# Spectral mixing and SiLU block: the first transform stage folds rows m and 47 - m, and runs as sixteen products between two pairs of chunks

## The chip, the core and the metric

The kernel runs on one core of one Trainium2 chip. The metric is the time of one execution in microseconds (us), measured on the device; a kernel's time is the median of its runs. The profile is one execution of the program, recorded by the hardware profiler. In it PE is the matmul engine (TensorE), PEld its loading of stationary operands, DVE the vector engine, ACT the scalar engine, POOL the GpSimd engine; SPq, ACTq and POOLq are those engines issuing DMA transfers.

## What is computed

```python
# x: (8, 3008, 256) fp32; filt_r, filt_i: (1505, 256); w_in: (256, 2048); w_out: (2048, 256)
X = np.fft.rfft(x, axis=1)                     # 3008 = 94 * 32 points, for each batch and channel
Y = X * (filt_r + 1j * filt_i)[None]
y = np.fft.irfft(Y, n=3008, axis=1)
x = y.reshape(24064, 256)
h = x @ w_in
g = h * (1.0 / (1.0 + np.exp(-h)))             # SiLU
out = g @ w_out
```

Everything is fp32. The forward transform is done in two stages: the first over 94 points (94 rows, 32 n' apart) for each of the 32 values of n', the second over the 32 n'. The two matrix products are done with seven products of quarters instead of eight (a Strassen scheme), which is where the tables A11, A12, S1 to S4 and A22 come from.

## The kernel before

The main loop has 8 batches x 48 steps. A step is one eighth of the hidden units (`NJP = 8`) of one pair of chunks of tokens; six pairs make a batch. A step has eight rounds. In each step `hidden` issues seven products for the first matrix and `project` seven for the second, for the step before. All four `acc` banks of a pair are copied out (`drain`) at the end of its eighth `project`.

```python
def hidden(step):                      # rounds 0 to 7, "yield" ends a round
    mm(xo, A11, yt[:, 0, 0:n], True);  nc.scalar.copy(out=sums[:, 0, 0:n], in_=xo)
    yield
    mm(zo, A12, yt[:, 1, 0:n], True);  combine(v, g[:, 0, 0:n], zo, sums[:, 0, 0:n], ALU.add)
    finish()                           # g[:, 6] and g[:, 7] of the step before
    yield
    mm(xo, S2, t[:, 2, 0:n], False);   nc.scalar.copy(out=sums[:, 1, 0:n], in_=xo);  silu(0)
    yield
    mm(yo, S1, t[:, 0, 0:n], True)
    yield
    mm(xo, S3, t[:, 1, 0:n], False);   nc.scalar.copy(out=sums[:, 2, 0:n], in_=xo)
    combine(v, g[:, 2, 0:n], yo, sums[:, 2, 0:n], ALU.add)
    yield
    yield
    mm(xo, A22, t[:, 3, 0:n], False);  silu(3, xo);  silu(2)
    yield
    mm(yo, S4, yt[:, 1, n:2 * n], False)
    combine(v, g[:, 1, 0:n], yo, sums[:, 1, 0:n], ALU.add);  silu(1)
    combine(v, g[:, 4:6, 0:n], g[:, 1:3, 0:n], g[:, 0:2, 0:n], ALU.subtract)
# drain(pair, i): acc bank i -> s, by ACT for even i and DVE for odd i; after i = 3 seven sums on GpSimd
```

The transform of batch b is cut into pieces, which are placed among the main loop's steps of the batch before (`put(step, round, piece)`; a piece is issued after that round's products). The pieces of the forward transform:

```python
def load_x(u):                         # u = 0..7: four n', rows 0..46 of both halves
    xs[u] = x_t[u % 2]                 # two tiles [128, 2, 2, C]
    for h in range(2):
        for r0, nr in ((0, 32), (32, N1 - 32)):
            queue.dma_start(out=xs[u][64 * h + r0:64 * h + r0 + nr], in_=...)

def sums(u):                           # even residues take the sum of the halves, odd ones the difference
    for par, op in ((0, ALU.add), (1, ALU.subtract)):
        nc.vector.tensor_tensor(out=ut[0:111, par], in0=xt[0:111, 0], in1=xt[0:111, 1], op=op)
    if b > 0 and u + 2 < 8:
        load_x(u + 2)

def stage1(u):                         # four products of 47 rows x 64 columns, 512 wide
    for par in range(2):
        for h in range(2):
            rows = slice(64 * h, 64 * h + N1)
            nc.tensor.matmul(out=ps[h][64 * par:64 * par + 64], lhsT=wf_t[rows, par],
                             rhs=ut[rows, par], start=True, stop=True)
    for h in range(2):
        evac(t1[:, h], ps[h])          # DVE and ACT by turns
    for par in range(2):
        nc.gpsimd.dma_start(out=d1[par]..., in_=t1[...])     # to DRAM, in transposed order

def forward(g):                        # second stage, g = 0..5: sixteen products of 64 x 32, 256 wide
    ...                                # load_t2(g) brings d1 back before it
def multiply(g, k): ...                # two DVE products 128x512 with the filter
def add(g, k): ...                     # two DVE sums 128x256
def inverse(g, n):                     # n = 2: thirty-two products of 32 x 64, 256 wide
    ps = [bank(b, f"pc_{b}_{g}_{j}", j // 2 if j % 2 == 0 else None) for j in range(4)]
    ...                                # two of its four banks are acc banks 0 and 1, free between two pairs
def even(g, i, n): ...                 # ACT copies bank 2 i out
def rows(g, i, n): ...                 # two DVE sums 128x512
def stage3(g): ...                     # last stage, g = 0..7: products of 48 x 64, 47 wide, two copies to y
```

```python
def plan(b, part):                     # b = 1..7
    at = STEPS * b                     # STEPS = 48
    put(at - 51, 0, part["load_x"], 0);  put(at - 51, 0, part["load_x"], 1)
    for u in range(8):
        put(at + u - (48 if u else 49), 5, part["sums"], u)
        put(at + u - 47, 3, part["stage1"], u)
    put(at - 39, 0, part["load_t2"], 0);  put(at - 39, 0, part["load_t2"], 1)
    ... # forward, multiply, add of g = 0..5 from -38 to -18
    for g, step in ((0, -32), (2, -24), (4, -16)):           # between two pairs of chunks
        put(at + step, 7, part["inverse"], g, 2)
        put(at + step, 7, part["even"], g, 0, 2)
        put(at + step + 1, 0, part["even"], g, 1, 2)
        put(at + step + 1, 5, part["rows"], g, 0, 2)
        put(at + step + 2, 3, part["rows"], g, 1, 2)
    ... # stage3: four at -11, -9, -6, -3, four at 9, 12, 15, 18
```

Batch 0 is transformed ahead of the main loop, together with the preparation of the weights.

Of the kernel before, what the change touches and what calls it, by code (L numbers as in the profile page):

```python
# [86 lines left out]
def dft_tables():  # L90

    wf = np.zeros((128, 2, 64))
    for par in range(2):
        for i, idx in enumerate(ORDER):
            ph = 2 * np.pi * (np.arange(N1) * (2 * idx + par) % 94) / 94
            for h in range(2):
                wf[64 * h:64 * h + N1, par, 2 * i] = np.cos(ph)
                wf[64 * h:64 * h + N1, par, 2 * i + 1] = -np.sin(ph)


    d = np.zeros((2, 2, 32, NS, 2, 32))
    n = np.arange(32)[:, None]
    for par in range(2):
        for i, idx in enumerate(ORDER):
            sp = 2 * idx + par
            kap = kept(sp)
            sg = np.where((kap - sp) % 94 == 0, 1.0, -1.0)
            k = np.where((kap - sp) % 94 == 0, kap, S - kap)
            th = 2 * np.pi * (n * k % S) / S
            d[par, 0, :, i, 0], d[par, 1, :, i, 0] = np.cos(th), np.sin(th)  # L110
            d[par, 0, :, i, 1], d[par, 1, :, i, 1] = -np.sin(th) * sg, np.cos(th) * sg


    e = np.zeros((4, 32, NG, 2, 2, 2, 32))
    n = np.arange(32)[None, :]
    for g in range(NG):
        for bank in range(2):
            for j in range(4):
                s = slot_residue(g, bank, j - j % 2)
                kap = kept(slot_residue(g, bank, j))  # L120
                sg = np.where((kap - s) % N1 == 0, 1.0, -1.0)[:, None]
                k = np.where((kap - s) % N1 == 0, kap, S - kap)[:, None]
                assert ((k - s) % 94 == (0 if j % 2 == 0 else N1)).all()
                th = 2 * np.pi * (n * k % S) / S
                e[j, :, g, bank, 0, 0], e[j, :, g, bank, 0, 1] = np.cos(th), np.sin(th)
# [12 lines left out]
    return (wf.astype(f32), wi.astype(f32), d.reshape(128, NS, 2, 32).astype(f32),  # L138
            e.reshape(128, NG, 2, 2, 64).astype(f32))


# [1 line left out]
def kernel(  # L143
# [9 lines left out]
    nc = tc.nc  # L153
    ctx.enter_context(tc.manual_schedule())

    wf_host, wi_host, d_host, e_host = dft_tables()
    wf_dram = nc.inline_tensor(wf_host, name="wf_tbl")
    wi_dram = nc.inline_tensor(wi_host, name="wi_tbl")
    d_dram = nc.inline_tensor(d_host, name="d_tbl")
    e_dram = nc.inline_tensor(e_host, name="e_tbl")  # L160
# [22 lines left out]
    accps = pool("accps", 1, PSUM)  # L183

    wf_t = cpool.tile([128, 2, 64], FP32)
    wi_t = cpool.tile([128, N1], FP32)
    d_t = cpool.tile([128, NS, 2, 32], FP32)
    e_t = cpool.tile([128, NG, 2, 2, 64], FP32)
# [2 lines left out]
    w_t = cpool.tile([128, 7, 2, NJP, 128], FP32)  # L191
    warm = cpool.tile([128, 1], FP32)
    bias_t = cpool.tile([128, 1], FP32)
    x_t = [xpool.tile([128, 2, 2, C], FP32, name=f"x{i}") for i in range(2)]

    def load_filters(first, last):
        for j in range(4):
# [35 lines left out]
    def spectral(b):  # L233
# [32 lines left out]
        def sums(u):  # L266
            if b > 0 or u % 3 == 0:
                ut = upool.tile([128, 2, 512], FP32, name=f"u_{b}_{u}", tag="u")
            else:
                if u == 1:  # L270
                    us["s"] = spool.tile([128, 2, 2, 512], FP32, name="u_s", tag="s")
                ut = us["s"][:, u % 3 - 1]
            xt = xs.pop(u)
            for par, op in ((0, ALU.add), (1, ALU.subtract)):
                nc.vector.tensor_tensor(out=ut[0:111, par], in0=xt[0:111, 0], in1=xt[0:111, 1], op=op)  # L275
            us[u] = ut
            if b > 0 and u + 2 < 8:
                load_x(u + 2)

        def stage1(u):  # L280
            ut = us.pop(u)
            if b > 0 or u < 2 or u > 5:
                t1 = tpool.tile([128, 2, 2, C], FP32, name=f"t1_{b}_{u}", tag="t")
            elif u < 4:
                t1 = typool.tile([128, 2, 2, C], FP32, name=f"t1_{b}_{u}", tag="ty")
            else:
                t1 = us["t1"][:, u - 4]
            ps = [bank(b, f"pa_{b}_{u}_{h}") for h in range(2)]
# [6 lines that stand above are left out]
                evac(t1[:, h], ps[h])  # L295
            for par in range(2):
                nc.gpsimd.dma_start(  # L297
                    out=d1[par].rearrange("s p n c -> (s p) n c")[:, 4 * u:4 * u + 4, :],
                    in_=t1[64 * par:64 * par + 2 * NS].rearrange("p h n c -> p (h n) c"))

        def load_t2(g):
            t2s[g] = tpool.tile([128, 4, C], FP32, name=f"t2_{b}_{g}", tag="t")
# [77 lines left out]
        def stage3(g):  # L380
# [17 lines left out]
            for h in range(2):  # L398
                evac(dst[:, :, h, n0:n0 + 4], ps[h])

        return dict(load_x=load_x, sums=sums, stage1=stage1, load_t2=load_t2, forward=forward,
                    multiply=multiply, add=add, inverse=inverse, even=even, rows=rows, load_t4=load_t4, stage3=stage3)

    pending = []

    def put(step, rnd, piece, *args):

        pending.append((step + rnd / ROUNDS, len(pending), lambda: piece(*args)))

    def plan(b, part):  # L410

        at = STEPS * b

        put(at - 51, 0, part["load_x"], 0)
        put(at - 51, 0, part["load_x"], 1)
        for u in range(8):
            put(at + u - (48 if u else 49), 5, part["sums"], u)
            put(at + u - 47, 3, part["stage1"], u)
        put(at - 39, 0, part["load_t2"], 0)
        put(at - 39, 0, part["load_t2"], 1)  # L420

        for g, places in enumerate((
# [6 lines left out]
            pieces = (("forward", g), ("multiply", g, 0), ("multiply", g, 1), ("add", g, 0), ("add", g, 1))  # L429
            for (step, rnd), (piece, *args) in zip(places, pieces):  # L430
                put(at + step, rnd, part[piece], *args)
        for g, step in ((0, -32), (2, -24), (4, -16)):

            put(at + step, 7, part["inverse"], g, 2)
            put(at + step, 7, part["even"], g, 0, 2)
            put(at + step + 1, 0, part["even"], g, 1, 2)
            put(at + step + 1, 5, part["rows"], g, 0, 2)
            put(at + step + 2, 3, part["rows"], g, 1, 2)
        put(at - 14, 5, part["load_t4"], 0)
        for g, step in enumerate((-11, -9, -6, -3)):  # L440
            put(at + step, 3, part["stage3"], g)
        plan_rest(b, part)

    def plan_rest(b, part):

        for g, (step, rnd) in enumerate(((9, 3), (12, 6), (15, 6), (18, 6))):
            put(STEPS * b + step, rnd, part["stage3"], 4 + g)

    pairs = [(b, half, c0, n) for b in range(B) for half in range(2) for c0, n in PAIRS]
# [228 lines left out]

    nc.sync.dma_start(out=wf_t, in_=wf_dram.ap())
    nc.gpsimd.memset(bias_t, -896.0)  # L680
    part = spectral(0)
    for u in range(8):
        part["load_x"](u)
# [14 lines left out]
    for g in range(NG):  # L698
        part["forward"](g)
        if g == 0:  # L700
            load_filters(4, 2 * NG)
            nc.sync.dma_start(out=wi_t, in_=wi_dram.ap())
        if g < 3:
            weights(1 + g)
        for k in range(2):
            part["multiply"](g, k)
        for k in range(2):
            part["add"](g, k)
        if 2 <= g < NG - 1:
            rounded(g)  # L710
        if g > 0:
            inverse_rows(part, g - 1)
# [18 lines left out]
    per = len(PAIRS) * 2  # L731


    combines = ((-2, 1), (6, 1), (14, 5), (22, 5), (26, 6), (38, 1))
    stores = (((10, 1), (10, 5)), ((19, 1), (23, 5)), ((31, 1), (31, 5)), ((35, 1), (35, 5)),
              ((43, 1), (43, 5)), ((50, 1), (51, 1)))
    for pair in range(len(pairs)):
# [55 lines left out]
```

## Time and profile before

| | |
|---|---|
| time, median of 3 runs | 2670.82 us (2669.16 to 2671.6) |
| span of the profiled execution | 2669.7 us |
| main loop starts (first `px<-y` product) | at 127.71 us |
| `pa` (first stage) matmul records, `L292` | 512 |
| DVE, `u<-x` sums, `L275` | 118 of mean 715 ns |
| `d<-t` transfers to DRAM issued by GpSimd, `L297` | 124, 526 ns each, 3.0 us to landing |
| `x<-in_x_dram` transfers issued by SP | 240, median 2.9 us (128 KB) and 2.7 us (60 KB) to landing |

A fp32 product appears in the profile as two records. A line of the timeline gives the start, the time until the last of its records ends, the engine, the line of the program, the operation, out<-in by tile names, the shape, and how many records were merged; records of PE overlap, so their durations must not be added up. What counts for PE is the distance from one start to the next. A window line gives a stretch of the span and, for each engine, its busy time and number of instructions, then the granted PE clock and the DMA engines' mean share and rate.

### The profile page before, as it was taken

The numbers are of one execution on the slowest core, as the hardware profiler recorded it, in microseconds if no ns is written. First come the engines' busy times: TensorE is split into PE (matmuls) and PEld (weight loads), VectorE is DVE, ScalarE is ACT, GpSimd is POOL, SyncE is SP. The second block draws the span as 40 slices with busy tenths as digits, with TensorE's granted clock in tenths as the row PEclk, the third lists the DMA queues.
The fourth block names the chain that finished last, engine by engine and source line by source line (L and its number), as shares of the span: only waits on it lengthen the run. The fifth ranks groups of instructions, "written<-read, shape, count | busy, mean of one in ns | idle before, by whom it ended". The sixth has DMA issues, their size and how long they took to land.

```text
span 2669.7 us, 47316 instructions
## 1 busy us (share of the span) xinstructions
PE 2582.3 (97%) x18432; PEld 2165.9 (81%) x18432; DVE 1683.3 (63%) x3554; ACT 1099.8 (41%) x3000; POOL 448.1 (17%) x653
## 2 busy tenths in 40 slices
PE   4589999999999999999999999999999999999998
PEld 1268888788887888888887888878888788888987
DVE  4886765667566665666656676566756667555554
ACT  1244444444444444444444444444444444444443
POOL 3541111211111111111101111021111111100100
PEclk9599999999999999999999999999999999999999
DMA  9732121421224211331123311132122421211000
GB/s 211 190 104 64 56 50 38 106 55 37 56 59 101 50 28 48 86 88 41 36 60 81 70 56 47 41 100 59 40 56 47 108 56 26 50 28 21 9 16 16
DMA packets 203616, 166.26 MB, mean 62 GB/s; under 512 B 120896, under 2 KB 175808, under 8 KB 203264
## 3 DMA queue, kind: packets, MB, share of 16 engines
q1 hardware_dynamic: 184728, 111.11, 18.6%
q0 software_dynamic: 14992, 47.46, 5.8%
q10 hardware_dynamic: 3672, 4.67, 0.7%
q8 instruction: 145, 2.38, 0.4%
q14 instruction: 79, 0.65, 0.1%
HBM read 88.17 MB, written 74.97 MB: 61 GB/s over the span
## 4 chain that ended last, share of the span: by engine, by line
PE 93%; DVE 2%; DMA 2%; SPq 1%; issue 1%; ACT 1%; POOL 0%; DVEq 0%; ACTq 0%
PE acc L543 42%; PE px L484 25%; PE pyz L484 18%; PE pd L391 3%; PE pa L292 2%; PE pb L315 2%; PE pc L348 2%; SPq L203 1%; DMA x<-in_x_dram 1%; DMA t<-d 1%; DVE g L455 0%; DMA d<-q 0%; DVE u L275 0%; DMA filt<-in_filt_i_dram 0%; DVE q L367 0%
## 5 line engine op out<-in xcount | busy, mean ns | idle before, releaser
L543 PE MATMUL acc<-g,w_t 128*128 128x256 f32 (+1 forms) x5376 | 1513.1, 375 | 0.4 <-DVE g L455 0.4
L543 PEld LDWEIGHTS acc<-g,w_t 128*128 128x128 f32 x5376 | 1022.2, 190 | 116.0 <-DVE g L455 0.8
L455 DVE TENSOR_TENSOR g<-pyz,abc 128x256 f32<-128x256 f32 (+1 forms) x1152 | 479.6, 416 | 553.9 <-ACT abc L505 321.3
L455 DVE TENSOR_TENSOR g<-g 128x256 f32<-128x256 f32 (+3 forms) x1152 | 617.4, 536 | 196.7 <-ACT g L488 183.6
L484 PE MATMUL px<-ty,w_t 128*128 128x256 f32 (+1 forms) x2304 | 690.3, 381 | 4.2 <-ACT abc L499 3.7
L488 ACT ACTIVATE g<-g 128x256 f32<-128x256 f32 (+1 forms) x1152 | 472.9, 411 | 231.6 <-DVE g L455 231.6
L484 PEld LDWEIGHTS px<-ty,w_t 128*128 128x128 f32 x2304 | 422.1, 190 | 118.5 <-issue 58.0
L455 POOL TENSOR_TENSOR s<-s 128x256 f32<-128x256 f32 (+1 forms) x329 | 259.1, 805 | 1318.5 <-DVE s L561 1262.3
L484 PE MATMUL pyz<-y,w_t 128*128 128x256 f32 (+1 forms) x1536 | 455.3, 378 | 1.7 <-DVE g L455 1.7
L484 PEld LDWEIGHTS pyz<-y,w_t 128*128 128x128 f32 x1536 | 283.3, 190 | 45.1 <-DVE g L455 5.6
L499 ACT COPY abc<-px 128x256 f32<-128x256 f32 (+1 forms) x384 | 141.5, 369 | 371.4 <-PE px L484 371.4
L488 ACT ACTIVATE g<-px 128x256 f32<-128x256 f32 (+1 forms) x384 | 146.1, 380 | 308.3 <-PE px L484 308.3
L505 ACT COPY abc<-px 128x256 f32<-128x256 f32 (+1 forms) x384 | 143.2, 373 | 296.1 <-PE px L484 295.9
L484 PE MATMUL px<-y,w_t 128*128 128x256 f32 (+1 forms) x768 | 228.8, 380 | 3.6 <-ACT g L488 2.7
L484 PE MATMUL pyz<-ty,w_t 128*128 128x256 f32 (+1 forms) x768 | 225.4, 375 | 0.7 <-DVE g L455 0.7
L484 PEld LDWEIGHTS px<-y,w_t 128*128 128x128 f32 x768 | 143.3, 190 | 29.2 <-issue 11.1
L484 PEld LDWEIGHTS pyz<-ty,w_t 128*128 128x128 f32 x768 | 145.5, 190 | 18.3 <-DVE g L455 1.8
L492 ACT COPY abc<-px 128x256 f32<-128x256 f32 (+1 forms) x384 | 134.9, 351 | 2.7 <-PE px L484 1.3
L213 DVE COPY y<-pd 128x376 f32<-128x376 f32 x64 | 51.3, 807 | 101.1 <-PE pd L391 101.1
L297 POOL DMA_DIRECT2D d<-t x124 | 64.7, 526 | 293.6 <-ACT abc L505 278.0
L391 PEld LDWEIGHTS pd<-wi_t,t 48*64 48x64 f32 x4096 | 69.5, 140 | 36.5 <-issue 29.2
L315 PE MATMUL pb<-t,d_t 64*32 64x256 f32 x1536 | 61.2, 408 | 37.4 <-DMA t<-d 18.9
(52 smaller groups left out, 1284.4 us busy)
## 6 DMA issues: line engine op xcount, KB each, us to landing
t<-d SPq DMA_DIRECT2D x96, 256.0 KB, 3.9
t<-d SPq DMA_DIRECT2D x128, 192.0 KB, 3.6
d<-t POOLq DMA_DIRECT2D x124, 192.0 KB, 3.0
d<-q POOLq DMA_DIRECT2D x85, 256.0 KB, 2.6
out_dram<-o SPq DMA_DIRECT2D x636, 32.0 KB, 1.8
x<-in_x_dram SPq DMA_DIRECT2D x120, 128.0 KB, 2.9
x<-in_x_dram SPq DMA_DIRECT2D x120, 60.0 KB, 2.7
raw<-in_moe_w_in_dram SPq DMA_DIRECT2D x16, 256.0 KB, 6.3
```

The source lines that it names most:

```text
L292: nc.tensor.matmul(out=ps[h][64 * par:64 * par + 64], lhsT=wf_t[rows, par], rhs=ut[rows, par], start=True, stop=True)
L297: nc.gpsimd.dma_start(out=d1[par].rearrange("s p n c -> (s p) n c")[:, 4 * u:4 * u + 4, :], in_=t1[64 * par:64 * par + 2 * NS].rearrange(" ...
L315: nc.tensor.matmul(out=ps[k][32 * j:32 * j + 32, ri, :], lhsT=d_t[rows, 4 * g + at, ri, :], rhs=t2[rows, at, :], start=True, stop=True)
L348: nc.tensor.matmul(out=ps[j][64 * k:64 * k + 64, a, :], lhsT=e_t[rows, g + a, k, ri, :], rhs=zs[k][rows, ri, :], start=(a == 0 and ri == 0 ...
L391: nc.tensor.matmul(out=ps[h][c0:c0 + 64, cb, i, :], lhsT=t4s[g][rows, i, 128 * cb + c0:128 * cb + c0 + 64], rhs=wi_t[rows, :], start=True, ...
L455: eng.tensor_tensor(out=out, in0=in0, in1=in1, op=op)
L484: nc.tensor.matmul(out=out, lhsT=w_t[:, c, 0, jp], rhs=rhs, start=start, stop=True, skip_group_check=True)
L488: nc.scalar.activation(out=g[:, k, 0:n], in_=g[:, k, 0:n] if src is None else src, func=AFT.Silu)
L492: nc.scalar.copy(out=sums[:, 0, 0:n], in_=xo)
L499: nc.scalar.copy(out=sums[:, 1, 0:n], in_=xo)
L505: nc.scalar.copy(out=sums[:, 2, 0:n], in_=xo)
L543: nc.tensor.matmul(out=acc[pair][i][:, h, 0:n], lhsT=w_t[:, c, 1, jp], rhs=g[:, k, 0:n], start=(jp == 0 and h == 0), stop=last, skip_group ...
```

## The change

From batch 2 on, six of the eight groups of four n' of the first stage are done in another way. The 94-point transform of real data has a symmetry: rows m and 47 - m have the same cosine and, but for the sign, the same sine. So rows m (0 to 23) and 47 - m are first summed and subtracted, and the product then needs 24 rows instead of 47. Four quarters of the partitions each hold two n', so that eight n' are done at a time (`f` = 0, 1, 2) with sixteen products of 24 rows x 32 columns: four sets of rows (`q`) times four tables (`k`: even and odd residues, cosine and sine). The remaining eight n' (`u` = 6, 7) stay as before, and so does the whole of batch 1.

The purpose is to have fewer passes through the matmul engine, and to have these passes between two pairs of chunks, where the accumulator banks 0 and 1 are free.

```diff
+    wq = np.zeros((128, 4, 32))                 # cosine and sine tables of 24 rows, for four quarters
...
-    x_t = [xpool.tile([128, 2, 2, C], FP32, name=f"x{i}") for i in range(2)]
+    x_all = xpool.tile([128, 2, 2, 2 * C], FP32)
+    x_t = [x_all[:, i] for i in range(2)]
...
-            if b > 0 and u + 2 < 8:
+            if b == 1 and u + 2 < 8:
                 load_x(u + 2)
...
+        def reverse_x():                        # DRAM to DRAM: rows 47 - m in the order of m
+            us["xr"] = dpool.tile([2, 24, 32 * C], FP32, name=f"xr_{b}", tag="xr")
+            nc.sync.dma_start(out=us["xr"][:, 1:24], in_=bass.AP(..., ap=[[32 * N1 * C, 2], [-32 * C, 23], [1, 32 * C]]))
+            for k in range(2):
+                nc.sync.dma_start(out=us["xr"][k, 0:1], in_=...)
+
+        def load_fold(f):                       # eight transfers
+            for q in range(4):
+                rows = slice(32 * q, 32 * q + 24)
+                nc.sync.dma_start(out=x_all[rows, 0], in_=...)         # rows m, two n'
+                nc.sync.dma_start(out=x_all[rows, 1], in_=us["xr"]...) # rows 47 - m
+
+        def fold(f, k):                         # k = 0..3
+            used = slice(0, 120)
+            if k == 0:
+                us["f"] = upool.tile([128, 2, 512], FP32, name=f"uf_{b}_{f}", tag="u")
+            xt, ut = x_all[used], us["f"][used]
+            todo = (((ut, xt[:, :, 0], xt[:, :, 1], ALU.add),),
+                    ((xt[:, :, 1], xt[:, :, 0], xt[:, :, 1], ALU.subtract),),
+                    ((xt[:, 0, 0], ut[:, 0], ut[:, 1], ALU.add),
+                     (xt[:, 1, 0], ut[:, 0], ut[:, 1], ALU.subtract)),
+                    ((ut[:, 0], xt[:, 0, 1], xt[:, 1, 1], ALU.subtract),
+                     (ut[:, 1], xt[:, 0, 1], xt[:, 1, 1], ALU.add)))
+            for out, in0, in1, op in todo[k]:
+                nc.vector.tensor_tensor(out=out, in0=in0, in1=in1, op=op)
+
+        def stage1_fold(f):
+            ut = us.pop("f")
+            rhs = x_all[:, 0, 0], x_all[:, 1, 0], ut[:, 0], ut[:, 1]
+            ps = [bank(b, f"pf_{b}_{f}_{q}", (0, 1, None, None)[q]) for q in range(4)]
+            for k in range(4):
+                for q in range(4):
+                    rows = slice(32 * q, 32 * q + 24)
+                    nc.tensor.matmul(out=ps[q][32 * k:32 * k + 32], lhsT=wq_t[rows, k], rhs=rhs[k][rows],
+                                     start=True, stop=True)
+
+        def evict_fold(f, q):
+            copy = nc.scalar.copy if q < 2 else nc.vector.tensor_copy
+            copy(out=us["tf"][:, q % 2], in_=us["ps"][q])
+            if q % 2:
+                for k in range(4):
+                    nc.gpsimd.dma_start(out=d1[k // 2, :, k % 2, n0:n0 + 4], in_=us["tf"][32 * k:32 * k + NS]...)
...
+        if b == 1:
             ...                                 # as before
+        else:
+            put(at - 72, 0, part["reverse_x"])
+            for f, step, load, places in ((0, -56, -66, ((-60, 3), (-60, 5), (-59, 5), (-58, 5))),
+                                          (1, -48, -55, ((-52, 3), (-52, 5), (-51, 5), (-50, 5))),
+                                          (2, -40, -44, ((-42, 5), (-41, 3), (-41, 5), (-40, 3)))):
+                put(at + load, 0, part["load_fold"], f)
+                for k, (fold_step, rnd) in enumerate(places):
+                    put(at + fold_step, rnd, part["fold"], f, k)
+                put(at + step, 7, part["stage1_fold"], f)
+                put(at + step, 7, part["evict_fold"], f, 0)
+                put(at + step + 1, 0, part["evict_fold"], f, 1)
+                put(at + step + 1, 5, part["evict_fold"], f, 2)
+                put(at + step + 1, 5, part["evict_fold"], f, 3)
+            for u, step in ((6, -46), (7, -45)):
+                put(at - 47, 0, part["load_x"], u)
+                put(at + step, 5, part["sums"], u)
+                put(at + step + 1, 3, part["stage1"], u)
-        put(at - 39, 0, part["load_t2"], 0)
+        put(at - 37, 0, part["load_t2"], 0)     # and of g = 1
-                ((-38, 3), (-37, 3), (-37, 5), (-36, 3), (-36, 5)),
-                ((-35, 3), (-35, 5), (-34, 3), (-33, 2), (-33, 5)),
+                ((-36, 3), (-36, 5), (-35, 3), (-35, 5), (-34, 5)),
+                ((-35, 6), (-34, 3), (-33, 3), (-33, 5), (-32, 1)),
...
-        for g, (step, rnd) in enumerate(((9, 3), (12, 6), (15, 6), (18, 6))):
+        for g, (step, rnd) in enumerate(((10, 3), (11, 3), (16, 3), (18, 6))):
             put(STEPS * b + step, rnd, part["stage3"], 4 + g)
...
+    nc.gpsimd.memset(x_all[96:128], 0.0)        # ahead of everything, in the preparation
+            nc.sync.dma_start(out=wq_t, in_=wq_dram.ap())
...
-    combines = ((-2, 1), (6, 1), (14, 5), (22, 5), (26, 6), (38, 1))
+    combines = ((-2, 1), (6, 1), (11, 5), (22, 5), (26, 6), (38, 1))
```

More of the change, by code (lines that the diff above doesn't have):

```diff
@@ L98, in dft_tables @@
                 wf[64 * h:64 * h + N1, par, 2 * i + 1] = -np.sin(ph)
+    wq = np.zeros((128, 4, 32))
+    m = np.arange(24)
+    for par in range(2):
+        for i, idx in enumerate(ORDER):
+            ph = 2 * np.pi * (m * (2 * idx + par) % 94) / 94
+            for q in range(4):
+                wq[32 * q:32 * q + 24, 2 * par, i] = np.where(m == 0, 0.5, np.cos(ph))
+                wq[32 * q:32 * q + 24, 2 * par + 1, i] = -np.sin(ph)
     d = np.zeros((2, 2, 32, NS, 2, 32))
@@ L137, in dft_tables @@
     f32 = np.float32
-    return (wf.astype(f32), wi.astype(f32), d.reshape(128, NS, 2, 32).astype(f32),
+    return (wf.astype(f32), wq.astype(f32), wi.astype(f32), d.reshape(128, NS, 2, 32).astype(f32),
             e.reshape(128, NG, 2, 2, 64).astype(f32))
@@ L154 @@
     ctx.enter_context(tc.manual_schedule())
-    wf_host, wi_host, d_host, e_host = dft_tables()
+    wf_host, wq_host, wi_host, d_host, e_host = dft_tables()
     wf_dram = nc.inline_tensor(wf_host, name="wf_tbl")
+    wq_dram = nc.inline_tensor(wq_host, name="wq_tbl")
     wi_dram = nc.inline_tensor(wi_host, name="wi_tbl")
@@ L185 @@
     wf_t = cpool.tile([128, 2, 64], FP32)
+    wq_t = cpool.tile([128, 4, 32], FP32)
     wi_t = cpool.tile([128, N1], FP32)
@@ L299, in stage1 @@
                     in_=t1[64 * par:64 * par + 2 * NS].rearrange("p h n c -> p (h n) c"))
+        def reverse_x():
+            us["xr"] = dpool.tile([2, 24, 32 * C], FP32, name=f"xr_{b}", tag="xr")
+            at = x.offset + b * S * C
+            nc.sync.dma_start(out=us["xr"][:, 1:24],
+                              in_=bass.AP(tensor=x.tensor, offset=at + 46 * 32 * C,
+                                          ap=[[32 * N1 * C, 2], [-32 * C, 23], [1, 32 * C]]))
+            for k in range(2):
+                nc.sync.dma_start(out=us["xr"][k, 0:1],
+                                  in_=bass.AP(tensor=x.tensor, offset=at + (1 - k) * 32 * N1 * C,
+                                              ap=[[32 * C, 1], [1, 32 * C]]))
@@ new lines, in load_fold @@
+        def load_fold(f):
+            at = x.offset + (b * S + 8 * f) * C
+            for q in range(4):
+                rows = slice(32 * q, 32 * q + 24)
+                n0 = (8 * f + 2 * q) * C
+                nc.sync.dma_start(out=x_all[rows, 0],
+                                  in_=bass.AP(tensor=x.tensor, offset=at + 2 * q * C,
+                                              ap=[[32 * C, 24], [32 * N1 * C, 2], [1, 2 * C]]))
+                nc.sync.dma_start(out=x_all[rows, 1],
+                                  in_=us["xr"][:, :, n0:n0 + 2 * C].rearrange("k m n -> m k n"))
@@ new lines, in stage1_fold @@
+        def stage1_fold(f):
[3 more added lines that the diff above has]
+            for k in range(4):
+                for q in range(4):
+                    rows = slice(32 * q, 32 * q + 24)
+                    nc.tensor.matmul(out=ps[q][32 * k:32 * k + 32], lhsT=wq_t[rows, k], rhs=rhs[k][rows],
+                                     start=True, stop=True)
+            us["ps"] = ps
@@ new lines, in evict_fold @@
+        def evict_fold(f, q):
+            if q % 2 == 0:
+                us["tf"] = tpool.tile([128, 2, 2, C], FP32, name=f"tf_{b}_{f}_{q}", tag="t")
+            copy = nc.scalar.copy if q < 2 else nc.vector.tensor_copy
+            copy(out=us["tf"][:, q % 2], in_=us["ps"][q])
+            if q % 2:
+                n0 = 8 * f + 2 * q - 2
+                for k in range(4):
+                    nc.gpsimd.dma_start(
+                        out=d1[k // 2, :, k % 2, n0:n0 + 4],
+                        in_=us["tf"][32 * k:32 * k + NS].rearrange("p q n c -> p (q n) c"))
@@ L399, in stage3 @@
                 evac(dst[:, :, h, n0:n0 + 4], ps[h])
-        return dict(load_x=load_x, sums=sums, stage1=stage1, load_t2=load_t2, forward=forward,
-                    multiply=multiply, add=add, inverse=inverse, even=even, rows=rows, load_t4=load_t4, stage3=stage3)
+        return dict(load_x=load_x, sums=sums, stage1=stage1, reverse_x=reverse_x,
+                    load_fold=load_fold, fold=fold, stage1_fold=stage1_fold, evict_fold=evict_fold,
+                    load_t2=load_t2, forward=forward, multiply=multiply, add=add, inverse=inverse, even=even, rows=rows, load_t4=load_t4, stage3=stage3)
     pending = []
@@ L412, in plan @@
         at = STEPS * b
[L414 to L418, printed above, removed]
-        put(at - 39, 0, part["load_t2"], 0)
-        put(at - 39, 0, part["load_t2"], 1)
+        if b == 1:
+            put(at - 51, 0, part["load_x"], 0)
+            put(at - 51, 0, part["load_x"], 1)
+            for u in range(8):
+                put(at + u - (48 if u else 49), 5, part["sums"], u)
+                put(at + u - 47, 3, part["stage1"], u)
+        else:
[16 more added lines that the diff above has]
+        put(at - 37, 0, part["load_t2"], 0)
+        put(at - 37, 0, part["load_t2"], 1)
         for g, places in enumerate((
[2 rows of a table removed]
[2 rows of a table added]
                 ((-29, 3), (-29, 5), (-28, 3), (-28, 5), (-27, 2)),
```

## The prediction, made before the changed kernel was run

> **What bounds the kernel now.** I read the page first: the busy times and the chain of work that ended last.
>
> ```profile
> PE 2582.3 (97%) x18432; PEld 2165.9 (81%) x18432; DVE 1683.3 (63%) x3554; ACT 1099.8 (41%) x3000; POOL 448.1 (17%) x653
> ...
> PE 93%; DVE 2%; DMA 2%; SPq 1%; issue 1%; ACT 1%; POOL 0%; DVEq 0%; ACTq 0%
> ```
>
> PE bounds it by both. But busy PE need not be PE at its peak, so the second view is the table of windows, first over the long stretches (preparation, steps of batch 0 with the weights still being prepared, the rest of that batch, a stretch of the next one), then over single steps, cut at the first product of each step.
>
> ```profile
> 0.00:127.70 127.70, 60.07 (x704) 27.64 (x705) 79.70 (x128) 25.12 (x44) 57.23 (x82) 0.76 0.83 205
> 127.70:197.94 70.24, 60.99 (x267) 42.67 (x267) 59.12 (x108) 30.62 (x76) 32.43 (x44) 0.93 0.37 102
> 197.94:459.15 261.21, 261.21 (x2026) 225.12 (x2025) 164.76 (x357) 110.34 (x306) 35.58 (x51) 1.00 0.22 53
> ...
> 465.01:472.27 7.26, 7.26 (x38) 5.44 (x38) 5.17 (x10) 3.05 (x9) 6.25 (x9) 1.00 0.03 8
> 530.41:537.67 7.26, 7.26 (x61) 5.72 (x60) 3.99 (x10) 2.42 (x8) 0.00 (x0) 1.00 0.45 83
> 537.67:543.71 6.04, 6.04 (x29) 5.32 (x28) 4.96 (x10) 2.42 (x8) 0.00 (x0) 1.00 0.63 139
> 459.15:465.01 5.86, 5.86 (x30) 5.21 (x29) 3.52 (x9) 3.31 (x10) 0.26 (x1) 1.00 0.22 66
> 675.92:690.11 14.19, 14.19 (x121) 11.84 (x120) 8.40 (x16) 7.01 (x19) 5.57 (x7) 1.00 0.17 28
> ```
>
> From 198 us on PE is busy in the whole of every window: no wait of another engine reaches it, so in the steady state time is removed only by removing PE work. A step without a piece takes 6.04 us: 14 products x 0.432 us (two records, started 0.216 us apart). With a first stage piece (465.01) it takes 7.26, with a second stage piece (530.41) also 7.26, so each costs 1.22. The step between two pairs with no piece (459.15) costs nothing extra: half its products are 240 wide and half 256, and 5.86 is the mean of 6.04 and 5.67. A step between two pairs with the inverse piece, taken with the one after it (675.92), takes 14.19, which is 2.10 over 12.09.
>
> Third, the timeline of PE around the first stage, to see what the 1.22 us are made of.
>
> ```profile
> 468.03 0.59 PE L543 MATMUL acc<-g,w_t 128*128 128x256 f32 x2
> 468.55 1.09 PE L292 MATMUL pa<-u,wf_t 47*64 47x512 f32 x8
> 469.57 0.70 PE L484 MATMUL px<-ty,w_t 128*128 128x256 f32 x2
> 470.11 1.03 PE L543 MATMUL acc<-g,w_t 128*128 128x256 f32 x4
> ```
>
> Each line is one merged group. In the trace's single records the eight of `pa` start in two groups of four, 0.48 us apart, with 7 ns between neighbours. So four products run at once, in two passes of 512 columns, 0.432 us each: 0.86. The other 0.35 us is entering and leaving: 0.09 before, 0.05 on the first pass, 0.09 after, 0.10 lost on the next product. The other pieces have the same sum. Second stage: 32 records, 8 at a time, 4 x 0.216 = 0.86, again 0.35 over. Inverse: 64 records, 8 at a time, 8 x 0.216 = 1.73, and 0.37 over. **A piece costs 0.36 us plus records / (tiles at once) x width's time.**
>
> [...] The trace has 4 (`pa`) and 8 (`pb`, `pc`) at once with 7 ns between starts; sixteen is not in it. [...] the trace has 0.68 (`z<-pb,filt`), with two in a row spaced 0.61. [...] the two `finish` sums take twice as long while GpSimd's seven sums after a drain run:
>
> ```profile
> 1003.87 1.81 DVE L455 TENSOR_TENSOR g<-g 128x256 f32<-128x256 f32 x2
> ...
> 1010.05 0.88 DVE L455 TENSOR_TENSOR g<-g 128x256 f32<-128x256 f32 x2
> ```
>
> **The change, part by part.**
>
> *Removed on PE:* `stage1` of u = 0..5 for six batches (2 to 7): 6 x 1.22 = 7.3 us a batch.
>
> *Added on PE:* three `stage1_fold` a batch. Each is 16 products, 32 records of 512 columns (0.432 us). With sixteen tiles at once that is two passes, 0.86 us, plus 0.36, plus 0.08 because the last of sixteen starts 12 x 7 ns later than the last of four: 1.30 us. It does the work of two u, which cost 2.44. Three cost 3.9 a batch.
>
> *Difference:* 7.3 - 3.9 = 3.4 us a batch, 20.3 us over six batches. Moving `stage3`, `load_t2`, `forward` and one `tokens` changes their number not at all.
>
> *DVE:* a `fold` is two pieces of one 1024-wide sum ([...]two 512-wide ones in a row take 1.28 in the timeline) and two pieces of two 512-wide ones, about 5.1 us for eight n'. Before it was two times 1.28. So 2.5 us more per f, 18 f: 45 us more DVE, 1683 to about 1728, beside PE. The pieces have the size of those placed today (`sums` 1.28, two products with the filter 1.3, `rows` 1.40), and two in a step at rounds 3 and 5 already occur without a wait (537.67, with 4.96 us of DVE in 6.04). None of the twelve falls into a step with GpSimd's sums: -60 to -58, -52 to -50 and -42 to -40 are before the pair ends.
>
> *Between two pairs:* evictions follow the pattern of the inverse: two ACT copies, at rounds 7 and 0, then DVE at round 5. There bank 0 and bank 1 are back before the next pair writes them, at a cost of 0.09 us in the next step, which my 0.36 contains.
>
> *GpSimd:* eight issues instead of four for eight n', 0.53 us each: 2.1 us more per f, 38 us in all, hidden, but they wait for the seven sums (5.8 us). For f = 2 that puts the last issue some 8.7 us after the products, its landing (3.0) at about 12, and `load_t2` is 12 us after; its landing (3.9) comes some 4 us before `forward`. Tight, but enough.
>
> *Transfers:* `load_fold` is eight issues of about 0.55 us (four `x` issues take 2.22 in the timeline): 4.4 us, and 2.9 to landing. `fold` comes 2.6 steps (16 us) or more later. `load_x` of u = 6 and 7 have 1.6 and 2.6 steps. `reverse_x` has six steps (37 us) for 1.5 MB; the queues' share is 0.22 in the mean.
>
> *Preparation:* GpSimd's clearing of 2048 columns (existing ones of 1024 take 0.94, so 1.9 us) precedes that of u = 1, which holds back the ACT queue's first loads; the table is one more transfer. I put 1 us on it, as this part is bound by transfers (share 0.83) and part of the delay is absorbed. Small waits of PE in the six batches: 0.5.
>
> **Sum:** 2670.8 - 20.3 + 1 + 0.5 = 2652.
>
> **Rivals.**
>
> *Sixteen at once don't happen.* If only eight of the sixteen run together, `stage1_fold` takes four passes, 1.73 + 0.36 = 2.1, and saves 0.3 each: 6 us in all, about 2666. For it: no sixteen in this trace. Against: `pb` has four different streams of moving data on the same rows and `pc` four sets of rows with four banks at once, so both halves of the demand are met today.
>
> *DVE becomes the bound.* In steps 0 to 7, where the weights are rounded on DVE and DVE is busy 59 of 70 us, PE waits 0.2 to 0.8 us in every first stage step for `g` or `abc`. If each of twelve pieces held PE by 0.3 us, 72 x 0.3 = 22 us would take back everything: about 2673. Against: steady steps with as much DVE work show none.
>
> *A transfer comes late.* [...]one late `x` or reversed row stalls `g` and then PE. 1 us in each of 18 `fold` would give 2670. SP [...] issues output stores in blocks of eight (4.3 us). The distances above speak against it.
>
> *A bank or table is late between the pairs.* Should ACT or DVE drain banks 0 and 1 late, each of 18 costs 0.3 to 0.6: 2657 to 2663. The inverse, with the same demand, shows no such wait.
>
> **Range and chances.** The main term is arithmetic on measured durations, and it can hardly be much larger: without the 0.08 us of late starts, 18 x 1.22 = 22 us. With the preparation free and no waits that gives 2649; 2 us for the spread of runs make the low end 2647. Upwards I allow for eight at a time, or half of one of the wait rivals: 2667. A gain over 2% (53 us) would need more than the whole first stage costs in those batches, 6 x 9.8 = 59 us, almost to vanish: 0.01. A loss over 2% would need waits of 4 us in each of 18 places: 0.02.
>
> **What would show it.** The step between pairs with `pf` should take 1.2 more than the bare 5.86, and the next about 0.1 more; the records of `pf` should start in two groups of sixteen, 0.43 to 0.48 apart. Four groups of eight mean the first rival. Steps with `fold` must stay at 6.04 or 5.67; if PE waits there for `g` or `abc`, it is DVE, and if DVE waits for `x` or `xr`, the transfers. A batch should last about 314.5 us between equal products instead of 317.9 (inverse pieces at 259.79 and 577.68), and the main loop should start at 127.7 to 129.5. I am wrong if the batch is shortened by less than 2 us.

## The result, and the profile after

| | before | changed |
|---|---|---|
| time, median | 2671.21 us (2669.16 to 2672.23, 4 runs) | 2659.36 us (2656.42 to 2661.87, 4 runs) |
| ratio | | 0.9956, 95% interval 0.9939 to 0.9973 |
| start of the main loop, in the profile | 127.71 us | 122.66 us |
| one batch (48 steps), batches 1 to 6 | 317.9 us | 314.8 to 316.3 us |
| DVE busy | 1683.3 us | 1728.3 us |

The change gains 11.9 us where 19 were predicted. The page of the changed kernel, busy times and chain:

```profile
PE 2566.0 (97%) x18720; PEld 2166.4 (82%) x18720; DVE 1728.3 (65%) x3590; ACT 1095.7 (41%) x3000; POOL 484.1 (18%) x726
...
PE 90%; DMA 3%; DVE 3%; SPq 1%; issue 1%; ACT 1%; POOL 0%; ACTq 0%; DVEq 0%; POOLq 0%
```

PE's busy time has gone down by 16 us, and the chain now has 90% of PE instead of 93%. The table of windows over single steps says where. In this order: a step with two `fold` pieces (-60), one with a `tokens` (DVE sums over the next pair's rows) and a `fold` (-58), the step between two pairs with `pf` (the banks of `stage1_fold`) and the one after it (-56 and -55), another step with `tokens` and `fold` (-50), and step 11 of batch 2. Columns: stretch, length, then PE, PEld, DVE, ACT and POOL busy with their numbers of instructions, PE clock, DMA share, GB/s.

```profile
698.41:704.45 6.04, 6.04 (x29) 5.31 (x28) 4.99 (x8) 2.42 (x8) 0.00 (x0) 1.00 0.34 57
711.77:717.82 6.05, 6.05 (x30) 5.32 (x29) 5.30 (x12) 2.43 (x8) 0.00 (x0) 1.00 0.05 10
725.13:737.93 12.80, 12.80 (x90) 10.68 (x88) 7.65 (x16) 6.72 (x19) 6.92 (x10) 1.00 0.31 73
763.18:768.85 5.67, 5.67 (x29) 5.28 (x28) 5.10 (x12) 2.33 (x8) 0.00 (x0) 1.00 0.00 0
847.06:856.25 9.19, 7.67 (x94) 6.41 (x93) 4.52 (x10) 3.09 (x9) 0.00 (x0) 1.00 0.56 118
```

Steps with `fold` take 6.05 and 5.67 us, as bare ones do. The step with `pf` and the next take 12.80, where bare ones take 5.86 + 5.67 = 11.53: one `stage1_fold` costs 1.27 us. The last line is the one that does not fit. A step with a last stage piece takes 7.32 us; this one takes 9.19, and PE is idle for 1.5 us of it.

The timeline of PE around one `stage1_fold` (start, length, operation, out<-in, number of records):

```profile
780.48 0.66 PE L363 MATMUL pf<-x_all,wq_t 24*32 24x512 f32 x8
780.53 0.66 PE L363 MATMUL pf<-uf,wq_t 24*32 24x512 f32 x8
780.93 0.63 PE L363 MATMUL pf<-x_all,wq_t 24*32 24x512 f32 x8
780.98 0.63 PE L363 MATMUL pf<-uf,wq_t 24*32 24x512 f32 x8
781.55 0.70 PE L580 MATMUL px<-y,w_t 128*128 128x256 f32 x2
```

The first sixteen start within 0.1 us and the second sixteen 0.45 us after the first: two passes with sixteen products at once.

Going through all 384 steps of both traces, the sum is this. In batches 1 to 5 the steps of the transform differ by what the change removed and added, -3.48 us a batch, 20.9 us for the six folded batches. Step 11 is longer than 7.32 us in all eight batches, by 3.5, 0.4, 1.9, 0.6, 1.5, 0.7, 2.1 and 1.5 us: 12.2 us. In batch 0 the granted clock is 0.84 in this step (214.37 to 225.17 us): from 222.19 to 223.87 it is 0.51, and two products of `acc` take these 1.68 us to the next start, where the same two took 0.86 in the step before, at 1.00. By 0.16 x 10.80 that is, as an estimate, 1.7 of its 3.5 us. Between batch 0's first ten steps and the last step of all, no other step has a new wait. The preparation is 5 us shorter in these two profiles; 0.9 of that is lost again in batch 0's first steps. The timeline around step 11 of batch 2, with SP's DMA issues, the DVE transposes of the rows that are stored, and the last stage on PE (`pd` is its bank):

```profile
805.36 0.59 SPq L338 DMA_DIRECT2D x_all<-xr  x1
...
842.58 0.77 DVE L669 STREAM_TRANSPOSE o<-s 128x256 f32<-128x256 f32 x2
...
843.38 4.92 SPq L677 DMA_DIRECT2D out_dram<-o  x8
848.35 0.93 SPq L455 DMA_DIRECT2D t<-d  x2
...
851.61 0.28 PE L469 MATMUL pd<-wi_t,t 48*64 48x47 f32 x2 [0.93 <-DMA t<-d]
852.48 1.14 PE L469 MATMUL pd<-wi_t,t 48*64 48x47 f32 x62 [0.59 <-DMA t<-d]
```

The products wait for their tile `t`, which `load_t4` brings from DRAM. `stage3` of g = 4 issues that load for g = 5. In the kernel before, g = 4 stood at step 9 and g = 5 at step 12; the change put them at steps 10 and 11, out of the steps of `pf` and its evictions (8 and 9) and of `forward` (12). So the load has lost two steps of lead in the program, and it has come behind the first eight output stores, placed at step 10 round 1. These wait for their rows: SP issues nothing from 805.95 us on until the transposes end at 843.35, and then takes 4.9 us for the eight. The load is held through both. The same place in the kernel before:

```profile
845.23 1.05 SPq L377 DMA_DIRECT2D t<-d  x2
...
851.93 3.67 SPq L581 DMA_DIRECT2D out_dram<-o  x8
```

There the load goes ahead of the stores.

### The profile page after: what moved, and what is told of

The parts are those of the page before. It is cut to its first block, busy times and chain, and to the rows that moved or that the text cites. A ratio compares the mean times of both kernels' runs of the same rounds, so it can differ in the third digit from the quotient of the medians.

```text
span 2657.1 us, 48172 instructions
## 1 busy us (share of the span) xinstructions
PE 2566.0 (97%) x18720; PEld 2166.4 (82%) x18720; DVE 1728.3 (65%) x3590; ACT 1095.7 (41%) x3000; POOL 484.1 (18%) x726
## 4 chain that ended last, share of the span: by engine, by line
PE 90%; DMA 3%; DVE 3%; SPq 1%; issue 1%; ACT 1%; POOL 0%; ACTq 0%; DVEq 0%; POOLq 0%
PE acc L639 41%; PE px L580 25%; PE pyz L580 18%; PE pd L469 2%; DMA t<-d 2%; PE pb L393 2%; PE pc L426 2%; DVE g L551 1%; SPq L677 1%; PE pf L363 1%; PE pa L308 1%; DVE u L291 0%; DMA x<-in_x_dram 0%; DMA filt<-in_filt_r_dram 0%; DMA e_t<-e_tbl 0%
## 5 line engine op out<-in xcount | busy, mean ns | idle before, releaser
L469 PE MATMUL pd<-wi_t,t 48*64 48x47 f32 x4096 | 80.3, 239 | 23.4 <-DMA t<-d 15.3
```

The source lines that it names most:

```text
L469: nc.tensor.matmul(out=ps[h][c0:c0 + 64, cb, i, :], lhsT=t4s[g][rows, i, 128 * cb + c0:128 * cb + c0 + 64], rhs=wi_t[rows, :], start=True, ...
```

## The experiments

**1. The load earlier.** Theory A: the lateness of this one load is the whole of the missing gain in the main loop. Rival B: something else in step 11 (banks, traffic).

```diff
-            if g < 7:
+            if g < 7 and g != 4:
                 load_t4(g + 1)
 ...
     def plan_rest(b, part):
+        put(STEPS * b + 7, 0, part["load_t4"], 5)
```

> Changed kernel, but the load of the sixth last-stage tile (load_t4 of g = 5) is issued at step 7 instead of at step 10 behind the first eight output stores. Theory A, the late load: this load stands in SP's queue behind eight store issues (4.9 us) and its use is one step later, so PE waits in step 11 of all eight batches (12.2 us in all by the trace). Then step 11 falls to 7.32 us in every batch and the time to about 2647 us (2659.4 - 12.2), ratio to before about 0.991. Rival B, the wait has another cause (banks, or more traffic on the DMA engines): step 11 stays at 7.9 to 10.8 us and the time at 2657 to 2661.

Measured: 2648.04 us (2646.72 to 2650.47), ratio to before 0.9919 (0.9905 to 0.9934). Step 11 of batch 2 in the table of windows, and SP's issues around it in the timeline:

```profile
846.35:853.67 7.32, 7.32 (x94) 6.23 (x92) 4.51 (x10) 3.08 (x9) 0.00 (x0) 1.00 0.34 58
```

```profile
805.31 0.84 SPq L455 DMA_DIRECT2D t<-d  x2
842.66 8.86 SPq L678 DMA_DIRECT2D out_dram<-o  x16
851.89 3.16 SPq L382 DMA_DIRECT2D t<-d  x4
```

Step 11 is 7.32 us in all eight batches, and 11.3 us of time are back. A holds and B falls. The issue is at 805 us, 14 us before step 7 starts (819.63), where the program now has it: SP has nothing left in front of it but the fold's loads, so it goes as far as its queue lets it. This speaks for the order in the queue, more than the step, as what counts.

**2. The stores later.** The same order by moving the other party.

```diff
-    stores = (((10, 1), (10, 5)), ...
+    stores = (((10, 4), (10, 5)), ...
```

> Changed kernel, with the first output stores of step 10 moved from round 1 to round 4, so that they stand behind the load of the sixth last-stage tile in SP's queue; the load stays where the program has it, one step ahead of its use. Theory A (the order in SP's queue holds the load): step 11 at 7.3 to 7.4 us, time about 2647 to 2649. Rival: one step is too short a distance in itself (issue 0.9 us and landing 3.6 us against some 7 us would speak against it) or the transfer is slow: step 11 keeps at least half of its 0.4 to 3.5 us of wait, time 2653 to 2659.

Measured: 2669.00 us (2666.03 to 2672.80), ratio 0.9995 (0.9986 to 1.0004). The expected time was missed by 20 us, though step 11 came out as A said: 7.32 us in every batch. The wait had moved one step on. Windows of steps 11 and 12 of batch 2 and of step 12 of batch 1, then the timeline of batch 2 (`pb` is the bank of `forward`):

```profile
849.74:857.06 7.32, 7.32 (x93) 6.24 (x92) 4.72 (x11) 3.07 (x9) 0.00 (x0) 1.00 0.35 59
857.06:868.37 11.31, 9.58 (x62) 6.59 (x61) 4.13 (x9) 2.43 (x8) 0.00 (x0) 0.85 0.79 180
540.36:549.94 9.58, 7.94 (x62) 5.77 (x60) 4.06 (x9) 2.42 (x8) 0.00 (x0) 1.00 0.84 177
```

```profile
808.43 0.93 SPq L455 DMA_DIRECT2D t<-d  x2
849.40 8.46 SPq L677 DMA_DIRECT2D out_dram<-o  x16
...
858.22 2.67 SPq L382 DMA_DIRECT2D t<-d  x4
...
861.93 0.59 PE L393 MATMUL pb<-t,d_t 64*32 64x256 f32 x2 [1.23 <-DMA t<-d]
```

With the stores out of its way the load is issued at 808.43 us, 34 us before step 10 starts (842.43), where the program still has it. So the order in the queue alone makes the wait, and whether one step between issue and use would be enough was not tried.

Sixteen stores now stand together, 8.5 us of issue, ahead of the second stage's first loads (`load_t2`, step 11 round 0), and `forward` waits for these in step 12, which is 2.3 to 6.3 us longer than 7.27 in batches 0 to 6. The block alone does not do it: in experiment 1 sixteen stores stand ahead of the same loads too, and step 12 is at most 0.4 us longer. There they start 3.7 us before step 11, here only 0.3, and the loads come 2.9 us later in the step. Nor is all of it waiting: in batches 0, 2, 5 and 6 the granted clock in step 12 is 0.75 to 0.85, and of the 4.0 us in batch 2, 0.15 x 11.31 = 1.7 are the clock's by the same estimate. Batches 1, 3 and 4, at a clock of 1.00, lose 2.3 to 2.5. Why the clock falls in some of these steps only is not shown.

It is the same mechanism on the next load in the queue. My expectation had looked at one load only, the error that the prediction made too.

**3. The moves alone.** Is the wait due to the moved pieces, or to the transfers that the fold adds? The kernel before, with the moves and no fold:

```diff
-        put(at - 39, 0, part["load_t2"], 0)          # and of g = 1
+        put(at - 37, 0, part["load_t2"], 0)
-                ((-38, 3), (-37, 3), (-37, 5), (-36, 3), (-36, 5)),
-                ((-35, 3), (-35, 5), (-34, 3), (-33, 2), (-33, 5)),
+                ((-36, 3), (-36, 5), (-35, 3), (-35, 5), (-34, 5)),
+                ((-35, 6), (-34, 3), (-33, 3), (-33, 5), (-32, 1)),
-        for g, (step, rnd) in enumerate(((9, 3), (12, 6), (15, 6), (18, 6))):
+        for g, (step, rnd) in enumerate(((10, 3), (11, 3), (16, 3), (18, 6))):
-    combines = ((-2, 1), (6, 1), (14, 5), ...
+    combines = ((-2, 1), (6, 1), (11, 5), ...
```

> Kernel before, with only the moved pieces of the change (last-stage pieces 4 to 7, first loads of the second stage, forward, multiply and add of groups 0 and 1, and one tokens piece), without any fold. Theory A: the moves alone bring the wait, 0.4 to 3.5 us in step 11 of each batch, 12 us in all: 2683 us, ratio about 1.0045. Rival C: the wait comes from the transfers that the fold adds: no wait in step 11, 2671 us.

Measured: 2678.56 us, ratio 1.0032 (1.0019 to 1.0045). Step 11 of batches 1 and 2:

```profile
537.65:548.75 11.10, 9.28 (x93) 7.64 (x92) 4.81 (x10) 3.21 (x9) 0.00 (x0) 0.85 0.68 142
859.33:867.47 8.14, 7.62 (x93) 6.42 (x92) 4.44 (x10) 3.08 (x9) 0.00 (x0) 1.00 0.59 125
```

The waits over 7.32 us sum to 10.4 us in the trace (1.7 of it is the lower clock, 0.85, in the first of these two lines), and the kernel is 7.8 us slower in its median. The moves make the wait without any fold; rival C falls. The amount varies from batch to batch, as it does in the changed kernel.

**4. The fold's DVE work doubled.** On the kernel of experiment 1, three of the four pieces of each fold are done twice, with the same result.

```diff
-            for out, in0, in1, op in todo[k]:
+            for out, in0, in1, op in todo[k] * (1 if k == 1 else 2):
```

> The kernel with the early load (2648.0 us), in which three of the four pieces of each fold (all but the in-place difference) are done twice: 3.7 us more DVE work for each f, 18 f, some 67 us more DVE in all, the result of each piece unchanged. Theory D, the fold lies wholly beside PE and has room to spare: steps with fold stay at 6.04 and 5.67 us, time 2646 to 2651. Rival, DVE is close to the bound there: PE waits for g in the steps -60 to -40, at least 0.3 us in each of the 54 doubled places, time above 2660.

Measured: 2692.84 us, 45 us slower than the kernel of experiment 1. Theory D falls in its second half. The 21 steps around one batch's folds (from -60 to the end of -40), in the kernel of experiment 1 and in this one:

```profile
697.70:832.88 135.18, 135.18 (x957) 115.27 (x955) 89.96 (x183) 59.48 (x165) 22.61 (x37) 1.00 0.26 61
```

```profile
701.54:844.25 142.71, 138.12 (x958) 114.71 (x956) 99.80 (x198) 59.62 (x165) 22.34 (x37) 1.00 0.25 58
```

DVE has 9.8 us more (57 in the whole run, where I had expected 67), and 7.5 us more appear in the time, though DVE is busy only 70% of the stretch. The timeline of the doubled kernel, at the turn from step -59 to -58, shows how:

```profile
714.74 1.89 DVE L354 TENSOR_TENSOR x_all<-uf 120x512 f32<-120x512 f32 x3
...
716.54 0.42 DVE L552 TENSOR_TENSOR g<-pyz,abc 128x256 f32<-128x256 f32 x1
...
717.02 0.70 PE L581 MATMUL pyz<-y,w_t 128*128 128x256 f32 x2 [0.71 <-DVE g L552]
```

The last sums of step -59 stand behind the doubled piece on DVE, and `pyz`, a bank of `hidden`, can't be written anew until they have read it. With single pieces, 1.2 to 1.3 us long, PE never waits there; with 2.5 us, ten steps with such pieces or just behind one are 0.2 to 1.4 us longer each. So the pieces are hidden, but the room in a place is less than one more piece.

**5. The preparation.** My prediction had put a loss of 1 us on GpSimd's clearing at the start; the profile had a gain of 5. The kernel before, with the joined tile and the clearing alone:

```diff
-    x_t = [xpool.tile([128, 2, 2, C], FP32, name=f"x{i}") for i in range(2)]
+    x_all = xpool.tile([128, 2, 2, 2 * C], FP32)
+    x_t = [x_all[:, i] for i in range(2)]
 ...
     nc.gpsimd.memset(bias_t, -896.0)
+    nc.gpsimd.memset(x_all[96:128], 0.0)
```

> Kernel before, with only the joined x tile and GpSimd's clearing of its last 32 partitions at the start. In the one profile of the changed kernel the main loop starts at 122.7 us instead of 127.7. Theory P: the clearing holds back the ACT queue's loads by 1.8 us, the first group's rows arrive sooner and the whole preparation gains: start at 122 to 124, time about 2666. Rival Q: the start scatters from execution to execution by some us: start within 126 to 129, or anywhere from 122 to 129 without system, time 2669 to 2672. My own prediction had a loss of 1 us here: 2672.

Measured: 2666.90 us, ratio 0.9985 (0.9977 to 0.9994); the main loop starts at 122.7 us. The gain is outside the spread of the runs. To learn whether the order makes it, the clearing was moved behind those of groups 1, 3 and 5, first in the kernel of experiment 1, where the two times can't be told apart:

```diff
-    nc.gpsimd.memset(x_all[96:128], 0.0)
     part = spectral(0)
     for u in range(8):
+        if u == 6:
+            nc.gpsimd.memset(x_all[96:128], 0.0)
         part["load_x"](u)
```

> The kernel with the early load (2648.0 us, main loop starts at 125.2 us in its profile; 122.7, 123.5 and 122.7 in the three others with the clearing first; 127.7 and 126.0 in the two without it), with GpSimd's clearing of the joined x tile moved behind those of groups 1, 3 and 5, just ahead of group 6, so that the ACT queue's first loads are not held back. Theory P, the hold-back of the ACT queue is what gains in the preparation: first sums again at about 7.6 us instead of 5.7, start of the main loop at 126 to 128, time 2650 to 2653. Rival, the joined tile gains it, or it is chance: first sums and start as with the clearing first, time about 2648.

Measured: 2649.16 us (2648.68 to 2651.23) against 2648.04 (2646.72 to 2650.47); first sums at 7.28 us instead of 5.67; start of the main loop 125.2 us in both profiles. Inconclusive, so the same edit was made in the kernel before, beside a second go of the clearing at the start, with more runs:

> Kernel before with the joined x tile, but its clearing behind those of groups 1, 3 and 5, so that the ACT queue's first loads are not held back; run beside a second go of the same kernel with the clearing first. Theory P, the hold-back gains the 3.9 us of e4: transfers at about 175 GB/s from 5 to 20 us of the span as in the kernel before (instead of 205 to 250), first sums at 7.3 to 7.6 us, time 2669 to 2671. Rival, the joined tile gains it whatever the order: time 2666 to 2667. Rival, chance: both kernels within 1 us of the kernel before.

> The kernel of e4 again (joined x tile, clearing first), beside e8 on one chip. Theory P: first sums at 5.7 to 6.0 us, time 2666 to 2668, some 3 to 4 us below the kernel before and e8. Chance: 2670 to 2672.

Measured: 2670.49 us with the clearing later, ratio 1.0000 (0.9991 to 1.0008), and 2666.92 with it first, ratio 0.9986 (0.9979 to 0.9993). Windows from 5 to 15 us of the span, clearing later and then clearing first (the last column is GB/s):

```profile
5.00:10.00 5.00, 2.05 (x10) 1.01 (x14) 2.77 (x5) 0.00 (x0) 1.41 (x2) 1.00 1.02 185
10.00:15.00 5.00, 5.00 (x20) 1.10 (x12) 3.62 (x6) 0.00 (x0) 0.00 (x0) 1.00 1.05 184
```

```profile
5.00:10.00 5.00, 3.53 (x14) 1.16 (x16) 2.85 (x5) 0.00 (x0) 1.35 (x2) 1.00 0.93 221
10.00:15.00 5.00, 4.69 (x18) 0.87 (x10) 4.91 (x9) 0.00 (x0) 0.00 (x0) 1.00 1.04 214
```

So in the kernel before the order does it, and the joined tile with a late clearing gains nothing. With the clearing first, the ACT queue's second load is issued at 3.7 instead of 1.9 us, the first rows come earlier (first sums at 5.5 instead of 7.2 us), the transfers run at a higher rate up to 20 us (283 instead of 202 GB/s in the last five), and 3.4 to 3.9 us are gained at the end. How the one leads to the other was not followed, and it does not always: in the kernel of experiment 1 the rates from 5 to 15 us differ likewise (239 and 211 GB/s against 173 and 175 with the clearing later), and hardly any gain is left. Over all eleven profiles the main loop starts at 122.2 to 125.2 us with the clearing first (seven) and at 125.2 to 127.7 us otherwise (four).

**6. A version that is better than both.** The kernel of experiment 1, with the second stage's first loads also ahead of the second stores:

```diff
-        put(at - 37, 0, part["load_t2"], 0)          # and of g = 1
+        put(at - 38, 4, part["load_t2"], 0)
```

> The kernel with the early load (2648.0 us), and in addition the first two loads of the second stage (load_t2 of groups 0 and 1) at step 10 round 4 instead of step 11 round 0, so that they stand ahead of the second eight output stores in SP's queue. Theory A, SP's order holds loads: the two waits left in step 12 (0.35 and 0.21 us in the profile) vanish, step 12 at 7.27 in all batches, time lower by about 0.5 us, within the spread: 2646 to 2649. Rival: the stores' later issue holds DVE's transposes and with them g: PE waits in steps 10 to 12, time above 2652.

Measured: 2648.53 us, ratio 0.9917 (0.9902 to 0.9932). The two waits left in step 12 are gone, which is too little to be seen in the time. It and experiment 1 are the best here: about 22 us below the kernel before, 11 below the change.

## Why the prediction was right, and where not

The time fell inside the range; the gain was 11.9 us where 18.8 were predicted. That it fell inside owes something to luck: the upper end had been set for eight products at a time or half of one of the rival waits, none of which came as described, and a loss that the prediction had left out was in part made up by a gain at the start that it had put down as a loss. By its steps:

- **The PE sum held.** A `stage1_fold` was put at 1.30 us and measured 1.27 (in the trace's single records 0.86 for two passes, 0.10 for the late starts, 0.30 for entering and leaving); the gain of 3.4 us a batch was measured as 3.48, 20.9 in all for 20.3. The rule "0.36 us plus records / (tiles at once) x width's time" carried over to sixteen tiles, which the trace of before did not have and the prediction had assumed, to 0.05 us. The rival of eight at a time fell with the two groups of sixteen.
- **The DVE sum held**: 45 us more were predicted and 45.0 measured, with no wait of PE in the steps with folds (6.05 and 5.67 us). The in-place 1024-wide sum took 1.22 us (median of 18 in the trace). But the argument for it, that steady steps show no wait at such a load, says less than I took it for. Experiment 4 shows that one more piece in the same place is paid for.
- **The step that failed** is "Moving `stage3`, `load_t2`, `forward` and one `tokens` changes their number not at all." It counted the moved pieces' work and not what they carry: `stage3(4)` issues the load for `stage3(5)`, and by the move this load came behind eight stores in SP's queue that wait for their rows, one step ahead of its use. The prediction worked out the distances of the new loads and of `load_t2`, not of the moved one. Mis-sized at 0, it measured 12.2 us in the trace (1.7 of it by the lower clock in batch 0) and 11.3 in the time (experiment 1). The rival "a transfer comes late" named the right kind of cause, and looked for it at the wrong tile and by way of DVE, whose pieces of `fold` waited for no row of `x` or `xr` in the trace.
- **The preparation** was put at +1 us and is -3.4 to -3.9 in the kernel before (experiment 5). The clearing does hold back the ACT queue, as predicted (its second load at 3.7 instead of 1.9 us); that this delays the whole was assumed, and the opposite is so.
- **The sum**: -20.9 + 12.2 - 3.6 = -12.3 us, for -11.9 measured. The 3.6 is carried over from the kernel before; in the kernel of experiment 1 the same order was worth 1.1 us, within the spread. The 0.5 us for other small waits did not occur in the steady state.
- **The signs named ahead**: the batch was to take about 314.5 us; it takes 314.8 to 316.3, and 314.4 where step 11's wait is taken off (313.1 in batch 6, which has one fold fewer). The main loop was to start at 127.7 to 129.5 us; it started at 122.7, which was the first sign that the preparation's term was wrong.
- **Two readings that don't hold as written**, neither of them in the sum: the waits of 0.2 to 0.8 us for `g` or `abc` are not in every first stage step of batch 0 but in steps 1 to 5 (step 6 waits 2.7 us, steps 7 and 8 not at all), and the 53 us of a 2% gain are not more than the 59 us of the first stage but nine tenths of them.

## What to carry to other kernels

When pieces of a schedule are moved, list for each what it issues for later pieces, and work out the distance of that load anew, in the order of the queue that issues it. Here a block of stores ahead of a load held it until the stored rows were ready (843.35 us in batch 2) and then for the block's issue time (4.9 us), and taking the block out of one load's way put it in the next one's (experiment 2, step 12 longer by 2.3 to 6.3 us). A piece's cost on the saturated engine could be summed from the trace to a few per cent (1.30 us for 1.27); for the engine beside it the free share said little (in experiment 4 a third of DVE was free, and 9.8 us more of it cost 7.5), and what counted was how long one piece may be between two results that the saturated engine needs (1.2 to 1.3 us was hidden there, 2.5 us was not).

## What the runs showed of the hardware that was not expected

At the start, SP and ACT both issue loads of the same kind. With ACT's held back by 1.8 us the rate from 5 to 15 us of the span was 214 to 221 GB/s instead of about 185, at about the same share of busy DMA engines (0.93 and 1.04 against 1.02 and 1.05), and the first sums came 1.7 us earlier. Which property of the transfers makes this difference (their order on the engines, or the rows that two loads touch at once) was not tried and stays open.

SP issued the same load 14 us (experiment 1) and 34 us (experiment 2) before the start of the step at which the program places it. In the changed kernel, where stores that waited for their rows stood ahead of it, it was issued at 848.35 us, 42 us after SP's last issue before these stores. A place in the program was here an order in the queue and not a time.
